# Masks added on TensorE, idle matmuls up front and earlier gates in an attention + expert kernel, with the loads of later batches re-hung to the new gates

## The chip, the cores and the metric

The kernel runs on one NeuronCore of a Trainium2 chip. The metric is the device time of one execution in microseconds (us); a profile's span of the same execution is about 1.6 us shorter. In the profile, PE is TensorE (it multiplies matrices into PSUM, its output memory), DVE is VectorE, ACT is ScalarE, and POOL is GpSimd. The granted clock is the share of TensorE's full clock that the profile shows. The DMA share is the time of all packets as a share of 16 DMA engines; it can exceed 1. The runs of the kernel before agree within 1%. Runs more than 1.5% above the fastest run of the same kernel are called slow.

## The reference, cut to what matters

Eight sentences (batches) of 576 positions, 8 heads of 64, pass through causal attention with a window of 64. The mean of the result over the positions picks one of eight experts for the whole sentence; the expert is a two-layer MLP with fp32 weights of 2 MB and 2 MB.

```python
scores = scale * np.matmul(q, k.transpose(0, 1, 3, 2))
mask = (rel >= 0) & (rel < window)                 # rel = row - column, window = 64
scores = np.where(mask, scores, -1000000000.0)
attn = ...softmax(scores)...;  x = attn @ v        # (B, S, H*D) = (8, 576, 512)
logits = x.mean(axis=1) @ w_gate                   # per sentence
e_idx = np.argmax(logits, axis=1)                  # one expert of 8 per sentence
h = np.maximum(x[mask] @ w1[e], 0.0)               # w1: 512 x 1024
out[mask] = gate_w * (h @ w2[e])                   # w2: 1024 x 512
```

So the weights of batch b can be loaded only when all of batch b's attention is done and its gate is known.

## The kernel before

Attention is cut into *units*: unit u = 5b + i is head pair i of batch b (i = 4 is the tail, positions 512 to 575). A unit has a transpose step T, a score step S and a value step A. The expert of a batch is cut into 18 *chunks*: nine of w1, nine of w2. Units and chunks are interleaved on TensorE. gate1(b) computes the logits, reads the index of the expert on GpSimd (POOL) and issues the loads of w1 and w2 there; gate2(b) broadcasts the gate's factor.

All loads of q, k, v, w1 and w2 are issued by POOL, because they change fp32 into a 2-byte type on the way. The Trainium skill, "DMA: Bandwidth & Descriptors", section "SWDGE vs HWDGE vs iDMA", says that a cast during DMA is tied to that path; the trace agrees in that all these loads are on one queue (q0, 30.94 MB). So POOL's program order is the order in which the loads start. In the trace they also landed in that order: behind gate 0, w1, w2, q and k had landed by 43.5, 49.2, 51.8 and 54.5 us (POOL's next issues wait for them).

```python
def load_qk(b, lo, hi): ...                 # 2 DMAs on nc.gpsimd, 512 KB each as stored in SBUF (2-byte)
def load_v(b, lo, hi): ...                  # 8 DMAs of 72 KB
def load_tail(b): ...                       # 2 DMAs of 64 KB

def unit_s(b, i):                           # scores; i < NP
    ... 8 matmuls into se, so ...
    nc.scalar.activation(out=pe, in_=se, func=AF.Exp, scale=scale)
    nc.scalar.activation(out=po, in_=so[:, :, 16:128], func=AF.Exp, scale=scale)
    nc.vector.tensor_tensor(out=pe, in0=pe, in1=mask, op=ALU.mult)
    nc.vector.tensor_tensor(out=po, in0=po, in1=mask[:, :, 0:112], op=ALU.mult)

def unit_a(b, i):                           # sums lb, values av: one PSUM buffer each
    ... ln(lb) and exp(-ln) on ScalarE, then on DVE:
    nc.vector.tensor_tensor_reduce(out=xm[:, i], in0=av, in1=rl, ..., accum_out=pool[b]...)

def gate1(b):
    ... 16 small matmuls gps <- pool, wg; glog, max, max_index on DVE ...
    nc.gpsimd.load(ereg, eidx[0:1, 0:1])
    nc.gpsimd.dma_start(out=w1t, in_=w1e[esl].squeeze(0))
    nc.gpsimd.dma_start(out=w2t, in_=w2e[esl].squeeze(0))
    ...

def moe(slot):                              # three slots a unit, LAG = 9
    t = slot - 3 * LAG
    want = min(len(todo), (t * NC) // (3 * NU)) if t > 0 else 0      # NC = 18, NU = 5
    ... issue chunks up to want ...

load_qk(1, 0, 8); load_v(1, 0, 4); load_tail(1)
unit_t(0, 0)
for u in range(n + 3):
    unit_t(u + 1); moe(3 * u); unit_s(u)
    if u >= 6 and (u - 6) % NU == 0:
        b = (u - 6) // NU
        gate1(b)
        if b == 0: load_qk(2, 0, 8); load_v(2, 0, 4); load_tail(2)
        if b + 3 < B: load_qk(b + 3, 0, 8); load_v(b + 3, 0, 4); load_tail(b + 3)
    if u >= 7 and (u - 7) % NU == 0: gate2((u - 7) // NU)
    moe(3 * u + 1); unit_a(u - 1); moe(3 * u + 2)
```

(Shortened: bounds are left out, units are named by number.) Note the load rule: behind gate b come q, k and v of batch b + 3, behind gate 0 also those of batch 2. A batch's data are thus asked for a whole batch before they are used.

The softmax here doesn't subtract the row's maximum and nothing guards it: scores larger than these inputs give would overflow.

Of the kernel before, what the change touches and what calls it, by code (L numbers as in the profile page):

```python
# [2 lines left out]
LAG=9  # L3
# [18 lines left out]
def kernel(  # L22
# [33 lines left out]
    NV = 3  # L56
# [30 lines left out]
    def load_v(b, lo, hi):  # L87
        vt = vbd[b % NV]
        for hh in range(2):
            for pr in range(lo, hi):  # L90
                nc.gpsimd.dma_start(  # L91
                    out=vt[64 * hh:64 * hh + 64, pr, :, 64 * hh:64 * hh + 64],
                    in_=v[b, 2 * pr + hh].rearrange("(j c) d -> c j d", c=64))

    nc.scalar.preload_act_table_set("natural_log_exp_and_others")
    ident = const.tile([128, 128], BF16)
    make_identity(nc, ident)
    load_qk(0, 0, 4)
    mb = const.tile([128, 4, 32], FP16)
    mt = const.tile([128, 2, 64], FP16)  # L100
    nc.vector.memset(mb, 1.0)
    nc.vector.memset(mt, 1.0)

    def zero(t, eng):
        for h in range(2):
            z = t[64 * h:64 * h + 64]
# [5 lines left out]

    zero(vbd[0], nc.vector)
    zero(kbd[0], nc.scalar)
    load_v(0, 0, 1)
    for p0 in (0, 64):
        m = mb[p0:p0 + 64]
        nc.gpsimd.affine_select(out=m, in_=m, compare_op=ALU.is_ge, fill=0.0,
                                base=0, pattern=[[1, 4], [4, 32]], channel_multiplier=-1)
        nc.gpsimd.affine_select(out=m, in_=m, compare_op=ALU.is_ge, fill=0.0,  # L120
                                base=63, pattern=[[-1, 4], [-4, 32]], channel_multiplier=1)
    load_v(0, 1, 2)
    load_qk(0, 4, 8)
    load_v(0, 2, 4)
    load_tail(0)
    for p0 in (0, 64):
        m = mt[p0:p0 + 64, 0]
        nc.gpsimd.affine_select(out=m, in_=m, compare_op=ALU.is_ge, fill=0.0,
                                base=-1, pattern=[[-1, 64]], channel_multiplier=1)
        m = mt[p0:p0 + 64, 1]  # L130
        nc.gpsimd.affine_select(out=m, in_=m, compare_op=ALU.is_ge, fill=0.0,
                                base=0, pattern=[[1, 64]], channel_multiplier=-1)
    mask = const.tile([128, 4, 128], FP16)
    for i in range(4):
        nc.vector.tensor_copy(out=mask[:, :, 32 * i:32 * i + 32], in_=mb)
    onesbd = const.tile([128, 128], FP16)
# [3 lines left out]
    ones1 = const.tile([1, 128], FP32)  # L140
    nc.vector.memset(ones1, 1.0)
    wg = const.tile([128, NP, E], FP32)
    nc.sync.dma_start(out=wg, in_=moe_w_gate.rearrange("(kb p) e -> p kb e", p=128))
    for i in range(2):
        zero(kbt[i].rearrange("q n (j d) -> q n j d", j=1), nc.scalar)
    zero(kbd[1], nc.scalar)
    zero(vbd[1], nc.scalar)
    zero(vbd[2], nc.scalar)

    tT = {}  # L150
    pt = {}
    xs = {}
# [3 lines left out]

    def unit_t(b, i):
        qm, km, qkt = qkv[b]
        if i < NP:
            tp = ps_t.tile([128, 2, 4, 128], BF16, tag="tp", name="tp")  # L160
            for (n, t) in ((0, qm), (1, km)):
                for r in range(4):
                    for hh in range(2):
                        p0 = 64 * hh
                        nc.tensor.transpose(tp[p0:p0 + 64, n, r], t[:, 2 * i + hh, ts(r, 64)], ident)  # L165
            qT = tpool.tile([128, 4, 128], BF16, tag="qT", name="qT", bufs=3)
            nc.vector.tensor_copy(out=qT, in_=tp[:, 0])  # L167
            kb = kbd[b % 2][:, i]
            for hh in range(2):
                p0 = 64 * hh  # L170
                (nc.vector.tensor_copy if KM == 'd' or (KM=='h' and hh==0) else nc.scalar.copy)(  # L171
# [3 lines left out]
        else:  # L175
            tp = ps_t.tile([128, NP, 128], BF16, tag="tp", name="tpt")
            for h in range(H):
                p0 = 64 * (h % 2)
                nc.tensor.transpose(tp[p0:p0 + 64, h // 2], qkt[:, h], ident)
# [280 lines left out]
```

## Time and profile before

| kernel before | value | view |
|---|---|---|
| time, 4 runs | 256.54 us median (255.12 to 257.44) | runs |
| span of the profiled run | 254.7 us | page |
| TensorE in work at 48-54 us | 0.64 of 6 us | table by stage |
| DMA share at 30-36 us | 0.01 | table by stage |
| gates 1 to 6 | 26.25 or 26.26 us apart | timeline |

The page's second part has the span in 40 slices of 6.4 us; digits are tenths of busy time, of the full clock (PEclk), and of the DMA engines.

```profile
PE   0487667059999999999999999999999999998893
...
PEclk9999955558999999999999999999999999999999
DMA  6999819999989999999999999999992199369923
```

Counted from 0: TensorE's slices 0 to 8 are not full, 7 is nearly empty and 8 half full, the clock stands at 0.5 in slices 5 to 8, and the DMA has one hole there, in slice 5. From slice 9 on TensorE is full until near the end. The table by stage (columns: window, its length, busy us of each engine with its instructions, granted clock, DMA share, GB/s) says the same in numbers:

```profile
30.00:36.00 6.00, 3.62 (x56) 2.79 (x52) 4.02 (x20) 2.38 (x6) 0.77 (x1) 0.68 0.01 3
...
48.00:54.00 6.00, 0.64 (x8) 0.40 (x8) 0.00 (x0) 0.00 (x0) 1.45 (x2) 0.50 1.54 192
...
90.00:96.00 6.00, 5.55 (x67) 3.24 (x66) 5.28 (x21) 3.11 (x8) 2.24 (x4) 1.00 1.96 173
```

Lines of the timeline (start, duration, engine, source line, operation, and in brackets the idle time before it and what ended it). The first is the issue of the first expert's w1; then batch 2's first transposes; then the first transposes of batches 3 and 4, which I call T(15) and T(20), with gate 2 between them:

```profile
35.22 0.77 POOL L294 DMA_DIRECT2D w1t<-in_moe_w_dram  x1 [8.63 <-DVE gw L305]
...
51.56 0.64 PE L165 MATMUL tp<-ident,qm 128*64 128x128 bf16 x8 [7.08 <-DMA qm<-in_q_dram]
...
54.21 0.64 PE L165 MATMUL tp<-ident,km 128*64 128x128 bf16 x8 [2.02 <-DMA km<-in_k_dram]
...
80.76 0.41 PE L165 MATMUL tp<-ident,qm 128*64 128x128 bf16 x8
...
93.13 0.55 PE L280 MATMUL gps<-wg,pool 128*1 128x8 f32 x16
...
107.02 0.41 PE L165 MATMUL tp<-ident,qm 128*64 128x128 bf16 x8
```

T(10) waits 7.1 us for q; T(15) and T(20) wait for nothing, their data have been there for over 12 us (k of batch 3 was issued at 57.4 and landed 8.8 us later, T(15) ran at 80.76; k of batch 4 landed at 94.2, T(20) ran at 107.02).

### The profile page before, as it was taken

How to read it: one execution, taken by the hardware profiler on the slowest of the kernel's cores; microseconds unless marked ns; L12 is line 12 of the kernel's file. 1: busy time of each engine (PE TensorE's matmuls, PEld its weight loads, DVE VectorE, ACT ScalarE, POOL GpSimd, SP SyncE). 2: the span in 40 equal slices, each digit the busy share in tenths (PEclk: the TensorE clock that was granted, in tenths of full speed). 3: DMA queues.
4: the chain of work that ended last, by engine and by line, in shares of the span. 5: the costliest groups of instructions: out<-in, count | busy, mean ns of one | idle time of the engine just before them, and what ended most of it. 6: DMA issues, size and time to landing. Idle time of an engine off the chain costs nothing.

```text
span 254.7 us, 5861 instructions
## 1 busy us (share of the span) xinstructions
PE 218.1 (86%) x2336; PEld 130.4 (51%) x2336; DVE 157.9 (62%) x444; ACT 132.1 (52%) x237; POOL 89.5 (35%) x128
## 2 busy tenths in 40 slices
PE   0487667059999999999999999999999999998893
PEld 0364455035565556565655665556555655554441
DVE  4569965136856796579747984698559854622411
ACT  8947644115565556646563656456555556522410
POOL 7995147158491129211931284125000200020000
PEclk9999955558999999999999999999999999999999
DMA  6999819999989999999999999999992199369923
GB/s 66 136 129 174 59 26 194 199 172 152 144 131 198 250 180 132 206 245 198 115 196 239 217 124 191 241 223 127 194 243 77 6 178 250 85 103 224 191 82 104
DMA packets 81995, 40.77 MB, mean 160 GB/s; under 512 B 48176, under 2 KB 73776, under 8 KB 81968
## 3 DMA queue, kind: packets, MB, share of 16 engines
q0 software_dynamic: 75552, 30.94, 102.4%
q1 hardware_dynamic: 6416, 9.46, 11.4%
q8 instruction: 18, 0.29, 0.4%
q14 instruction: 9, 0.07, 0.1%
HBM read 61.88 MB, written 9.44 MB: 280 GB/s over the span
## 4 chain that ended last, share of the span: by engine, by line
DMA 49%; PE 29%; POOL 10%; issue 5%; DVE 3%; ACT 2%; POOLq 1%; DVEq 0%
DMA km<-in_k_dram 35%; PE po L357 9%; PE ph L335 8%; DMA vbd_95<-in_v_dram 8%; DMA w2t<-in_moe_w_dram 7%; POOL vbd_94 L91 3%; PE tp L165 2%; POOL qm L76 2%; POOL w2t L295 1%; POOL qkt L83 1%; PE lb L231 1%; PE po L368 1%; PE ph L342 1%; PE av L235 1%; PE av L241 1%
## 5 line engine op out<-in xcount | busy, mean ns | idle before, releaser
L335 PE MATMUL ph<-xm,w1t 128*128 128x512 f16 x256 | 64.5, 386 | 0.9 <-DMA w1t<-in_moe_w_dram 0.9
L357 PE MATMUL po<-w2t,hm 128*128 128x512 f16 x256 | 62.7, 380 | 1.0 <-DMA w2t<-in_moe_w_dram 1.0
L249 DVE CUSTOM_DVE_ANT_0 xm<-av,rl 128x512 f16<-128x512 f32 x32 | 22.1, 692 | 46.7 <-ACT rl L248 46.7
L321 ACT ACTIVATE hm<-ph,gwb 128x512 f16<-128x512 f32 x32 | 22.0, 687 | 30.7 <-PE ph L335 30.5
L335 PEld LDWEIGHTS <-w1t 128*128 128x128 f16 x256 | 22.4, 99 | 22.5 <-DMA w1t<-in_moe_w_dram 1.2
L357 PEld LDWEIGHTS <-hm 128*128 128x128 f16 x256 | 21.7, 98 | 22.6 <-DMA w2t<-in_moe_w_dram 1.1
L91 POOL DMA_DIRECT2D vbd_95<-in_v_dram x24 | 17.7, 771 | 34.1 <-DMA w2t<-in_moe_w_dram 14.7
L165 PE MATMUL tp<-ident,qm 128*64 128x128 bf16 x256 | 14.6, 242 | 17.6 <-DMA qm<-in_q_dram 12.9
L201 ACT ACTIVATE pe<-se 128x512 f16<-128x512 f32 x32 | 19.0, 594 | 20.3 <-PE se L197 20.3
L323 DVE TENSOR_SCALAR hm<-ph,gwb 128x512 f16<-128x512 f32 x32 | 23.8, 743 | 5.9 <-PE ph L335 5.5
L294 POOL DMA_DIRECT2D w1t<-in_moe_w_dram x8 | 6.2, 774 | 55.0 <-DVE gw L305 54.9
L247 ACT ACTIVATE ln<-lb 128x512 f32<-128x512 f32 x32 | 19.1, 597 | 11.3 <-PE lb L237 11.0
L91 POOL DMA_DIRECT2D vbd_94<-in_v_dram x24 | 17.8, 774 | 18.8 <-DMA w2t<-in_moe_w_dram 6.1
L165 PEld LDWEIGHTS <-qm 128*64 128x64 bf16 x256 | 9.0, 118 | 26.6 <-DMA qm<-in_q_dram 14.3
L171 DVE COPY kbd_98<-tp 64x512 bf16<-64x512 bf16 x32 | 21.9, 683 | 0.2
L171 DVE COPY kbd_97<-tp 64x512 bf16<-64x512 bf16 x32 | 21.9, 683 | 0.2
L167 DVE COPY qT<-tp 128x512 bf16<-128x512 bf16 x32 | 13.4, 419 | 12.6 <-PE tp L165 12.6
L91 POOL DMA_DIRECT2D vbd_96<-in_v_dram x16 | 11.8, 762 | 26.1 <-DMA w2t<-in_moe_w_dram 11.5
L248 ACT ACTIVATE rl<-ln 128x512 f32<-128x512 f32 x32 | 20.2, 630 | 1.0
L231 PE MATMUL lb<-pe,onesbd 128*128 128x512 f16 x32 | 13.3, 414 | 6.9 <-DVE glog L286 4.6
L362 DVE COPY ob<-po 128x512 f32<-128x512 f32 x16 | 11.0, 689 | 13.0 <-PE po L357 12.8
L214 ACT ACTIVATE pp<-st 128x512 f16<-128x512 f32 x8 | 4.8, 597 | 26.1 <-PE st L211 26.1
(109 smaller groups left out, 363.7 us busy)
## 6 DMA issues: line engine op xcount, KB each, us to landing
w1t<-in_moe_w_dram POOLq DMA_DIRECT2D x8, 1024.0 KB, 9.4
w2t<-in_moe_w_dram POOLq DMA_DIRECT2D x8, 1024.0 KB, 16.3
out_dram<-ob SPq DMA_DIRECT2D x32, 256.0 KB, 6.5
qm<-in_q_dram POOLq DMA_DIRECT2D x7, 512.0 KB, 19.5
km<-in_k_dram POOLq DMA_DIRECT2D x7, 512.0 KB, 21.4
vbd_94<-in_v_dram POOLq DMA_DIRECT2D x24, 72.0 KB, 6.4
vbd_95<-in_v_dram POOLq DMA_DIRECT2D x24, 72.0 KB, 8.5
vbd_96<-in_v_dram POOLq DMA_DIRECT2D x16, 72.0 KB, 15.1
```

The costliest lines, as they stand in the source:

```text
L91: nc.gpsimd.dma_start(out=vt[64 * hh:64 * hh + 64, pr, :, 64 * hh:64 * hh + 64], in_=v[b, 2 * pr + hh].rearrange("(j c) d -> c j d", c=64))
L165: nc.tensor.transpose(tp[p0:p0 + 64, n, r], t[:, 2 * i + hh, ts(r, 64)], ident)
L171: (nc.vector.tensor_copy if KM == 'd' or (KM=='h' and hh==0) else nc.scalar.copy)(out=kb[p0:p0 + 64, :, p0:p0 + 64].rearrange("q j (p r) - ...
L201: nc.scalar.activation(out=pe, in_=se, func=AF.Exp, scale=scale)
L231: nc.tensor.matmul(out=lb, lhsT=onesbd, rhs=pe, start=True, stop=False, skip_group_check=True)
L247: nc.scalar.activation(out=ln, in_=lbf, func=AF.Ln)
L248: nc.scalar.activation(out=rl, in_=ln, func=AF.Exp, scale=-1.0)
L249: nc.vector.tensor_tensor_reduce(out=xm[:, i], in0=av.rearrange("q r p -> q (r p)"), in1=rl, scale=1.0, scalar=0.0, op0=ALU.mult, op1=ALU.add,
L321: nc.scalar.activation(out=o, in_=i, func=AF.Relu, scale=g)
L323: nc.vector.tensor_scalar(out=o, in0=i, scalar1=g, scalar2=0.0, op0=ALU.mult, op1=ALU.max)
L335: nc.tensor.matmul(out=ph, lhsT=w1t[:, kb, ts(ft, 128)], rhs=xm[:, kb], start=(kb == 0), stop=(kb == 3))
L357: nc.tensor.matmul(out=po, lhsT=hm[:, fb, ts(r, 128)], rhs=w2t[:, fb], start=(fb == 0), stop=(fb == 7))
```

## The change

Its intent: bring the first expert's weights forward, since all later loads queue behind them. Masks of the first five units become matmuls that add -30000 to masked scores ahead of the exponential (DVE is spared two multiplies a unit). Twelve idle matmuls at the start are to raise TensorE's clock. Gate 0 moves into its batch's last unit, gate 1 from unit 11 to the end of unit 9, and the first 12 chunks of expert 0 are placed by hand among units 7 to 9. The set-up is reordered. The loads hang on the gates, so their rule is rewritten too. Cut to its core:

```diff
-LAG=9
+WU=12;PB=5;KA=set(range(0));C1=12;A2=42
...
+    for i in range(WU):
+        nc.tensor.matmul(out=wps, lhsT=warm[:, 0:128], rhs=warm, start=True, stop=True)
...
+                if pm and j == 0:
+                    nc.tensor.matmul(out=se, lhsT=ident, rhs=maskb, start=True, stop=False,
+                                     skip_group_check=True)
...
-            nc.vector.tensor_tensor(out=pe, in0=pe, in1=mask, op=ALU.mult)
-            nc.vector.tensor_tensor(out=po, in0=po, in1=mask[:, :, 0:112], op=ALU.mult)
+            if b * NU + i >= PB:
+                nc.vector.tensor_tensor(out=pe, in0=pe, in1=mask, op=ALU.mult)
+                nc.vector.tensor_tensor(out=po, in0=po, in1=mask[:, :, 0:112], op=ALU.mult)
...
     def moe(slot):
-        t = slot - 3 * LAG
-        want = min(len(todo), (t * NC) // (3 * NU)) if t > 0 else 0
+        if slot < 30:
+            return
+        if slot < A2:
+            want = C1 + (NC - C1) * (slot - 30) // (A2 - 30)
+        else:
+            want = min(len(todo), NC + (slot - A2) * NC // (3 * NU))
...
+        if u == 4:
+            ops += [("S", 4), ("E", 4), ("A", 3), ("A", 4), ("Tp", 5), ("G1", 0), ("GR", 0),
+                    ("Te", 5), ("T", 6), ("S", 5), ("E", 5), ("G2", 0)]
...
+        if u == 9:
+            ops += [("C", 1), ("A", 9), ("C", 3), ("G1", 1), ("GR", 1), ("C", 2), ("T", 10), ("G2", 1)]
...
+        g = u > 11 and (u - 6) % NU == 0
...
+    LD = {0: lambda: loads(2), 1: lambda: loads(3), 2: lambda: (loads(4), qk(5)),
+          3: lambda: (vt(5), loads(6)), 4: lambda: loads(7), 5: lambda: None,
+          6: lambda: None, 7: lambda: None}
```

LD[b] is what is loaded right behind gate b's weights. From slot 42 (unit 14) on, the pace of the chunks is the same as before: (slot - 27) * 18 / 15 and 18 + (slot - 42) * 18 / 15 are equal.

More of the change, by code (lines that the diff above doesn't have):

```diff
@@ L87, in load_v, with zero @@
     def load_v(b, lo, hi):
-        vt = vbd[b % NV]
-        for hh in range(2):
-            for pr in range(lo, hi):
+        for pr in range(lo, hi):
+            for hh in range(2):
+                p0 = 64 * hh
                 nc.gpsimd.dma_start(
-                    out=vt[64 * hh:64 * hh + 64, pr, :, 64 * hh:64 * hh + 64],
+                    out=vbd[b % NV][p0:p0 + 64, pr, :, p0:p0 + 64],
                     in_=v[b, 2 * pr + hh].rearrange("(j c) d -> c j d", c=64))
     nc.scalar.preload_act_table_set("natural_log_exp_and_others")
-    ident = const.tile([128, 128], BF16)
-    make_identity(nc, ident)
-    load_qk(0, 0, 4)
-    mb = const.tile([128, 4, 32], FP16)
-    mt = const.tile([128, 2, 64], FP16)
-    nc.vector.memset(mb, 1.0)
-    nc.vector.memset(mt, 1.0)
-    def zero(t, eng):
+    def zero(t, eng, lo=0, hi=None):
         for h in range(2):
-            z = t[64 * h:64 * h + 64]
+            z = t[64 * h:64 * h + 64, lo:hi]
             z = z.rearrange("q n j d -> q (n j) d")[:, :, 64 - 64 * h:128 - 64 * h]
@@ L111, in zero @@
                 eng.memset(z.bitcast(U32), 0)
+    ident = const.tile([128, 128], BF16)
+    mb = const.tile([128, 4, 32], FP16)
+    mt = const.tile([128, 2, 64], FP16)
+    onesbd = const.tile([128, 128], FP16)
+    ones1 = const.tile([1, 128], FP32)
+    warm = const.tile([128, 512], BF16)
+    mask = const.tile([128, 4, 128], FP16)
+    maskb = const.tile([128, 4, 128], BF16)
+    mtb = const.tile([128, 2, 64], BF16)
+    wg = const.tile([128, NP, E], FP32)
+    load_qk(0, 0, 2)
+    nc.vector.memset(warm, 0.0)
@@ new lines @@
+    nc.vector.memset(ident, 0.0)
+    nc.vector.memset(mb, 1.0)
+    nc.vector.memset(mt, 1.0)
+    nc.gpsimd.affine_select(out=ident, in_=ident, compare_op=ALU.not_equal, fill=1.0,
+                            base=0, pattern=[[-1, 128]], channel_multiplier=1)
+    nc.sync.dma_start(out=wg, in_=moe_w_gate.rearrange("(kb p) e -> p kb e", p=128))
+    wps = ps_m.tile([128, 512], FP32, tag="mo", name="wps")
+    for i in range(WU):
+        nc.tensor.matmul(out=wps, lhsT=warm[:, 0:128], rhs=warm, start=True, stop=True)
@@ L113 @@
+    m = mb[0:64]
+    nc.gpsimd.affine_select(out=m, in_=m, compare_op=ALU.is_ge, fill=0.0,
+                            base=0, pattern=[[1, 4], [4, 32]], channel_multiplier=-1)
+    nc.gpsimd.affine_select(out=m, in_=m, compare_op=ALU.is_ge, fill=0.0,
+                            base=63, pattern=[[-1, 4], [-4, 32]], channel_multiplier=1)
+    load_qk(0, 2, 8)
+    zero(kbd[0], nc.scalar)
     zero(vbd[0], nc.vector)
-    zero(kbd[0], nc.scalar)
     load_v(0, 0, 1)
-    for p0 in (0, 64):
-        m = mb[p0:p0 + 64]
-        nc.gpsimd.affine_select(out=m, in_=m, compare_op=ALU.is_ge, fill=0.0,
-                                base=0, pattern=[[1, 4], [4, 32]], channel_multiplier=-1)
-        nc.gpsimd.affine_select(out=m, in_=m, compare_op=ALU.is_ge, fill=0.0,
-                                base=63, pattern=[[-1, 4], [-4, 32]], channel_multiplier=1)
+    m = mt[0:64, 0]
@@ L122 @@
+    nc.gpsimd.affine_select(out=m, in_=m, compare_op=ALU.is_ge, fill=0.0,
+                            base=-1, pattern=[[-1, 64]], channel_multiplier=1)
+    m = mt[0:64, 1]
+    nc.gpsimd.affine_select(out=m, in_=m, compare_op=ALU.is_ge, fill=0.0,
+                            base=0, pattern=[[1, 64]], channel_multiplier=-1)
     load_v(0, 1, 2)
-    load_qk(0, 4, 8)
+    load_tail(0)
     load_v(0, 2, 4)
-    load_tail(0)
-    for p0 in (0, 64):
-        m = mt[p0:p0 + 64, 0]
-        nc.gpsimd.affine_select(out=m, in_=m, compare_op=ALU.is_ge, fill=0.0,
-                                base=-1, pattern=[[-1, 64]], channel_multiplier=1)
-        m = mt[p0:p0 + 64, 1]
-        nc.gpsimd.affine_select(out=m, in_=m, compare_op=ALU.is_ge, fill=0.0,
-                                base=0, pattern=[[1, 64]], channel_multiplier=-1)
@@ L133 @@
-    mask = const.tile([128, 4, 128], FP16)
-    for i in range(4):
-        nc.vector.tensor_copy(out=mask[:, :, 32 * i:32 * i + 32], in_=mb)
-    onesbd = const.tile([128, 128], FP16)
     nc.vector.memset(onesbd, 0.0)
@@ L139 @@
     nc.vector.memset(onesbd[64:128, 64:128], 1.0)
-    ones1 = const.tile([1, 128], FP32)
     nc.vector.memset(ones1, 1.0)
-    wg = const.tile([128, NP, E], FP32)
-    nc.sync.dma_start(out=wg, in_=moe_w_gate.rearrange("(kb p) e -> p kb e", p=128))
-    for i in range(2):
-        zero(kbt[i].rearrange("q n (j d) -> q n j d", j=1), nc.scalar)
+    nc.vector.tensor_copy(out=mb[64:128], in_=mb[0:64])
+    for i in range(4):
+        nc.vector.tensor_copy(out=mask[:, :, 32 * i:32 * i + 32], in_=mb)
+    nc.vector.tensor_scalar(out=maskb, in0=mask, scalar1=-1.0, scalar2=30000.0,
+                            op0=ALU.add, op1=ALU.mult)
+    zero(vbd[1], nc.vector)
     zero(kbd[1], nc.scalar)
-    zero(vbd[1], nc.scalar)
-    zero(vbd[2], nc.scalar)
+    zero(kbt[0].unsqueeze(2), nc.scalar)
+    zero(kbt[1].unsqueeze(2), nc.scalar)
     tT = {}
     pt = {}
+    sps = {}
     xs = {}
@@ L155, with unit_tp @@
     wts = {}
+    tps = {}
     def unit_t(b, i):
+        unit_tp(b, i)
+        unit_te(b, i)
+    def unit_tp(b, i):
         qm, km, qkt = qkv[b]
         if i < NP:
-            tp = ps_t.tile([128, 2, 4, 128], BF16, tag="tp", name="tp")
+            if b == 0 and i % 2:
+                tp = ps_m.tile([128, 2, 4, 128], BF16, tag="mo", name="tp")
+            else:
+                tp = ps_t.tile([128, 2, 4, 128], BF16, tag="tp", name="tp")
             for (n, t) in ((0, qm), (1, km)):
@@ L165, in unit_t, with unit_te @@
                         nc.tensor.transpose(tp[p0:p0 + 64, n, r], t[:, 2 * i + hh, ts(r, 64)], ident)
+            tps[b, i] = tp
+        else:
+            tp = ps_t.tile([128, NP, 128], BF16, tag="tp", name="tpt")
+            for h in range(H):
+                p0 = 64 * (h % 2)
+                nc.tensor.transpose(tp[p0:p0 + 64, h // 2], qkt[:, h], ident)
+            tps[b, i] = tp
+    def unit_te(b, i):
+        tp = tps.pop((b, i))
+        if i < NP:
             qT = tpool.tile([128, 4, 128], BF16, tag="qT", name="qT", bufs=3)
@@ L170, in unit_t @@
                 p0 = 64 * hh
-                (nc.vector.tensor_copy if KM == 'd' or (KM=='h' and hh==0) else nc.scalar.copy)(
+                (nc.scalar.copy if hh and b * NU + i in KA else nc.vector.tensor_copy)(
                     out=kb[p0:p0 + 64, :, p0:p0 + 64].rearrange("q j (p r) -> q j p r", r=4),
@@ L175, in unit_t @@
         else:
-            tp = ps_t.tile([128, NP, 128], BF16, tag="tp", name="tpt")
-            for h in range(H):
-                p0 = 64 * (h % 2)
-                nc.tensor.transpose(tp[p0:p0 + 64, h // 2], qkt[:, h], ident)
             qT = tpool.tile([128, NP, 64], BF16, tag="qTt", name="qTt")
@@ L193, in unit_s @@
             so = ps_s.tile([128, 4, 128], FP32, tag="so", name="so")
+            pm = b * NU + i < PB
             for j in (0, 2, 4, 6, 1, 3, 5, 7):
@@ L196, in unit_s, with unit_e @@
                 dst = (so if j % 2 else se)[:, :, 16 * j:16 * j + w]
-                nc.tensor.matmul(out=dst, lhsT=kb[:, j], rhs=qT[:, :, 16 * j:16 * j + w],
-                                 start=True, stop=True, skip_group_check=True)
+                if pm and j == 0:
+                    nc.tensor.matmul(out=se, lhsT=ident, rhs=maskb, start=True, stop=False,
+                                     skip_group_check=True)
+                if pm and j == 1:
+                    nc.tensor.matmul(out=so[:, :, 16:128], lhsT=ident, rhs=maskb[:, :, 0:112],
+                                     start=True, stop=False, skip_group_check=True)
+                nc.tensor.matmul(out=dst, lhsT=kb[:, j], rhs=qT[:, :, 16 * j:16 * j + w],
+                                 start=not pm, stop=True, skip_group_check=True)
+            sps[b, i] = (se, so)
+        else:
+            sp = ps_s.tile([128, NP, 2, 64], FP32, tag="se", name="st")
+            pm = b * NU + i < PB
+            if pm:
+                nc.tensor.matmul(out=sp, lhsT=ident,
+                                 rhs=mtb.unsqueeze(1).broadcast_to([128, NP, 2, 64]),
+                                 start=True, stop=False, skip_group_check=True)
+            for n in range(NP):
+                nc.tensor.matmul(out=sp[:, n, 0], lhsT=kbd[b % 2][:, n, 7], rhs=qT[:, n],
+                                 start=not pm, stop=True, skip_group_check=True)
+                nc.tensor.matmul(out=sp[:, n, 1], lhsT=kbt[b % 2][:, n], rhs=qT[:, n],
+                                 start=not pm, stop=True, skip_group_check=True)
+            sps[b, i] = sp
+    def unit_e(b, i):
+        if i < NP:
+            se, so = sps.pop((b, i))
             pe = apool.tile([128, 4, 128], FP16, tag="pe", name="pe", bufs=3)
@@ L202, in unit_s @@
             nc.scalar.activation(out=po, in_=so[:, :, 16:128], func=AF.Exp, scale=scale)
-            nc.vector.tensor_tensor(out=pe, in0=pe, in1=mask, op=ALU.mult)
-            nc.vector.tensor_tensor(out=po, in0=po, in1=mask[:, :, 0:112], op=ALU.mult)
+            if b * NU + i >= PB:
+                nc.vector.tensor_tensor(out=pe, in0=pe, in1=mask, op=ALU.mult)
+                nc.vector.tensor_tensor(out=po, in0=po, in1=mask[:, :, 0:112], op=ALU.mult)
             pt[b, i] = (pe, po)
         else:
-            sp = ps_s.tile([128, NP, 2, 64], FP32, tag="se", name="st")
-            for n in range(NP):
-                nc.tensor.matmul(out=sp[:, n, 0], lhsT=kbd[b % 2][:, n, 7], rhs=qT[:, n],
-                                 start=True, stop=True, skip_group_check=True)
-                nc.tensor.matmul(out=sp[:, n, 1], lhsT=kbt[b % 2][:, n], rhs=qT[:, n],
-                                 start=True, stop=True, skip_group_check=True)
+            sp = sps.pop((b, i))
             pp = apool.tile([128, NP, 2, 64], FP16, tag="pp", name="pp")
             nc.scalar.activation(out=pp, in_=sp, func=AF.Exp, scale=scale)
-            nc.vector.tensor_tensor(
-                out=pp, in0=pp,
-                in1=mt.unsqueeze(1).broadcast_to([128, NP, 2, 64]), op=ALU.mult)
+            if b * NU + i >= PB:
+                nc.vector.tensor_tensor(
+                    out=pp, in0=pp,
+                    in1=mt.unsqueeze(1).broadcast_to([128, NP, 2, 64]), op=ALU.mult)
             pt[b, i] = pp
@@ L299, in gate1, with gate_w @@
                                 scalar2=None, op0=ALU.mult)
+        gates[b] = (glog, gnm)
+    def gate_w(b):
+        glog, gnm = gates[b]
         gex = gpool.tile([1, E], FP32, tag="gex", name="gex")
@@ L390, in moe @@
     def moe(slot):
-        t = slot - 3 * LAG
-        want = min(len(todo), (t * NC) // (3 * NU)) if t > 0 else 0
+        if slot < 30:
+            return
+        if slot < A2:
+            want = C1 + (NC - C1) * (slot - 30) // (A2 - 30)
+        else:
+            want = min(len(todo), NC + (slot - A2) * NC // (3 * NU))
         while done[0] < want:
@@ L395, in moe, with loads @@
             done[0] += 1
+    def loads(b):
+        if b < B:
+            load_qk(b, 0, 8)
+            load_v(b, 0, 4)
+            load_tail(b)
+    n = len(units)
+    ops = []
+    for u in range(n + 3):
+        b = u // NU
+        if u == 4:
+            ops += [("S", 4), ("E", 4), ("A", 3), ("A", 4), ("Tp", 5), ("G1", 0), ("GR", 0),
+                    ("Te", 5), ("T", 6), ("S", 5), ("E", 5), ("G2", 0)]
+            continue
+        if u == 5:
+            ops += [("T", 7), ("S", 6), ("E", 6), ("A", 5)]
+            continue
+        if u == 6:
+            ops += [("T", 8), ("S", 7), ("E", 7), ("A", 6)]
+            continue
+        if u == 7:
+            ops += [("T", 9), ("C", 1), ("S", 8), ("E", 8), ("C", 1), ("A", 7), ("C", 1)]
+            continue
+        if u == 8:
+            ops += [("C", 1), ("S", 9), ("E", 9), ("C", 1), ("A", 8), ("C", 1)]
+            continue
+        if u == 9:
+            ops += [("C", 1), ("A", 9), ("C", 3), ("G1", 1), ("GR", 1), ("C", 2), ("T", 10), ("G2", 1)]
+            continue
+        ops += [("T", u + 1), ("M", 3 * u), ("S", u)]
+        g = u > 11 and (u - 6) % NU == 0
+        if g:
+            ops += [("G1", b - 1)]
+        ops += [("E", u)]
+        if g:
+            ops += [("GR", b - 1)]
+        ops += [("M", 3 * u + 1)]
+        if u != 10:
+            ops += [("A", u - 1)]
+        if g:
+            ops += [("G2", b - 1)]
+        ops += [("M", 3 * u + 2)]
@@ L397, with qk, vt @@
+    fn = {"T": unit_t, "Tp": unit_tp, "Te": unit_te, "S": unit_s, "E": unit_e, "A": unit_a}
+    def qk(b):
+        load_qk(b, 0, 8)
+    def vt(b):
+        load_v(b, 0, 4)
+        load_tail(b)
+    LD = {0: lambda: loads(2), 1: lambda: loads(3), 2: lambda: (loads(4), qk(5)),
+          3: lambda: (vt(5), loads(6)), 4: lambda: loads(7), 5: lambda: None,
+          6: lambda: None, 7: lambda: None}
     with tc.manual_schedule():
-        load_qk(1, 0, 8)
-        load_v(1, 0, 4)
-        load_tail(1)
@@ L401 @@
         unit_t(0, 0)
-        n = len(units)
-        for u in range(n + 3):
-            if u + 1 < n:
-                unit_t(*units[u + 1])
-            moe(3 * u)
-            if u < n:
-                unit_s(*units[u])
-            if u >= 6 and (u - 6) % NU == 0:
-                b = (u - 6) // NU
-                gate1(b)
-                if b == 0:
-                    for c in (2,):
-                        load_qk(c, 0, 8)
-                        load_v(c, 0, 4)
-                        load_tail(c)
-                if b + 3 < B:
-                    load_qk(b + 3, 0, 8)
-                    load_v(b + 3, 0, 4)
-                    load_tail(b + 3)
-            if u >= 7 and (u - 7) % NU == 0:
-                gate2((u - 7) // NU)
-            moe(3 * u + 1)
-            if 1 <= u <= n:
-                unit_a(*units[u - 1])
-            moe(3 * u + 2)
+        loads(1)
@@ new lines @@
+        zero(vbd[2], nc.gpsimd)
+        for (op, x) in ops:
+            if op == "M":
+                moe(x)
+            elif op == "G1":
+                if x < B:
+                    gate1(x)
+                    LD[x]()
+            elif op == "C":
+                for _ in range(x):
+                    todo[done[0]]()
+                    done[0] += 1
+            elif op == "GR":
+                if x < B:
+                    gate_w(x)
+            elif op == "G2":
+                if x < B:
+                    gate2(x)
+            elif 0 <= x < n:
+                fn[op](*units[x])
+            if (op, x) == ("S", 1):
+                nc.vector.tensor_copy(out=mt[64:128], in_=mt[0:64])
+                nc.vector.tensor_scalar(out=mtb, in0=mt, scalar1=-1.0, scalar2=30000.0,
+                                        op0=ALU.add, op1=ALU.mult)
```

## The prediction

> **What bounds the kernel now.**
> 1. Up to 60 us: waiting. The table by stage shows TensorE busy 0.64 of 6 us at 48-54. Batch 2's first transposes wait 7.1 us for q and 2.0 for k (waits of TensorE). Before that the DMA idles: at 30-36 its share is 0.01, from the landing of batch 1's last loads (29) to the issue of expert weights w1(0) at 35.2. The gate was late: sums at 30.9, glog copied at 33.4, behind copies and mask multiplies (2.6) on DVE. The granted clock is 0.50 at 36-54.
> 2. 60-222: TensorE. Busy over 98% of 100-200; one batch takes 26.26 us (gate matmuls at 93.13, 119.39, 145.65).
> 3. The tail: gate 7 at 221.6, w2(7) lands 242.2.
> The DMA is nearly as full in stage 2: w1, w2, q, k and v of a batch with its outputs take about 26.5 us.
>
> **What the change does.** Masks as matmuls for five units: DVE 3.3 us a unit falls to 2.5; TensorE gains two 512-column matmuls a unit (0.21 us each warm). Twelve idle matmuls (0.43 cold) overlap the first loads. The Trainium skill, "TensorE: Matmul & The Clock Gate", part 1, gives about 3.4 us of activity before full clock; the trace agrees roughly (54.8-59.3 dense, then full rate). Gate 0 moves to about 24, but w1(0) sits on POOL behind batch 1's loads and a memset, so I put its issue at 27.5 (35.2 before). Expert 0's first 12 chunks fill the wait for batch 2. Gate 1 moves from 66.9 to about 48. But qk(3) now come after w(1), and batch 4 after gate 2's w(2): a prefetch is one batch shallower until gate 3.
>
> **On the critical path.** From unit 14 on the chunk pacing is the same as before, so only what unit 14's and unit 19's transposes gain counts.
> - T(15), 80.8 before: it waits for k(3). DMA, with the durations of before: issue 27.5, +19 k(2), +5.4 v(2), +12 w(1), +5.5 qk(3), +2 outputs: about 71. TensorE would be there at 66.
> - Gate 2: +12.4, about 84; w1(2) issued at 86, with the DMA idle since about 77.
> - T(20), 107.0 before: TensorE wants it 13.9 us after gate 2, but w(2) and qk(4) take 19 to 22 us from issue. Landing about 106; a new stall of some 7 us, then a cold restart (about 2 us).
> The 10 us lead at T(15) is given back at T(20). From there the gate broadcast placed right after a unit's sums must wait for ln to read the same PSUM bank (about 0.6 us a batch lost), the earlier glog copy saves 0.44.
>
> **Predicted: 256 us** (8 in 10: 250 to 262.5); faster by over 2% 0.2, within 0.65, slower 0.15.
>
> **What would show it.** Right: w1(0) issued at 26-30; no long TensorE gap at 45-55; T(15) at 69-74; among TensorE's waits k or q of batch 4, 5 us or more at 97-107, granted clock 0.5 after it; a DMA trough at 77-86; T(20) within 3 us of 107; then 26.3 us a batch. Wrong: T(20) at 102 or earlier (gain kept), or w1(0) still after 32.
>
> **What would make it wrong.** DMA faster than the durations of before : T(15) and T(20) move with it, and 5 us are possible. Or the early steps slower: mask constants late on POOL, gate 1 after 52, a clock that stays low through units 5-13; then over 260.

## The result, and the profile after

Measured: 272.86 us median of 4 runs (270.27 to 274.62), against 256.54 for the kernel before. The ratio is 1.061, 95% interval 1.050 to 1.071. Ratios here are the mean time of one kernel's fast runs over that of the other's fast runs of the same rounds, so not quite the ratio of the medians quoted. The profiled run (274.62, span 273.0) was the slowest of the four; the three fast ones are at 270 or more as well, and a fast trace of a kernel that is identical up to gate 3 (f_gate3 below) has gates 0 to 4 at the same times to within 0.6 us. The third hole below is seen in this run alone; f_gate3 shows the same kind of hold-up one batch later, in a fast run.

```profile
PE   7495598979439995089999999489999999998983
...
PEclk9888569988968999669999999979999999999998
DMA  5999299969995099999299999999998079639913
```

Slices are 6.8 us here. The hole of before (slices 7 and 8 there) is gone, but there are three new ones in TensorE's row: slices 10 and 11, 15 and 16, and 25. The DMA's row is half full in slice 12 and empty in 13, shortly before the second. TensorE's waits, summed (total, times, longest):

```profile
PE tp L185 <- DMA qm<-in_q_dram: 15.0, 3, 7.7
PE tp L185 <- DMA km<-in_k_dram: 6.9, 3, 2.7
PE ph L388 <- DMA w1t<-in_moe_w_dram: 5.6, 2, 4.8
```

And the timeline, with the same events as before: w1(0), T(15), gate 2, the issue of w1(2), T(20), and the third hole.

```profile
30.84 0.77 POOL L343 DMA_DIRECT2D w1t<-in_moe_w_dram  x1 [3.13 <-DVE qT L198]
...
76.53 0.64 PE L185 MATMUL tp<-ident,qm 128*64 128x128 bf16 x8 [5.05 <-DMA qm<-in_q_dram]
...
79.92 0.64 PE L185 MATMUL tp<-ident,km 128*64 128x128 bf16 x8 [2.75 <-DMA km<-in_k_dram]
...
92.55 0.54 PE L329 MATMUL gps<-wg,pool 128*1 128x8 f32 x16
...
95.03 0.77 POOL L343 DMA_DIRECT2D w1t<-in_moe_w_dram  x1 [12.78 <-PE av L290]
...
114.17 0.64 PE L185 MATMUL tp<-ident,qm 128*64 128x128 bf16 x8 [7.71 <-DMA qm<-in_q_dram]
...
116.91 0.64 PE L185 MATMUL tp<-ident,km 128*64 128x128 bf16 x8 [2.11 <-DMA km<-in_k_dram]
...
178.66 1.71 PE L388 MATMUL ph<-xm,w1t 128*128 128x512 f16 x4 [4.79 <-DMA w1t<-in_moe_w_dram]
```

The table by stage shows what went on between gate 1's loads and gate 2's:

```profile
84.00:90.00 6.00, 6.00 (x62) 3.52 (x61) 3.98 (x9) 4.43 (x9) 0.00 (x0) 1.00 0.11 22
90.00:96.00 6.00, 5.51 (x75) 3.49 (x73) 5.26 (x22) 3.76 (x8) 0.97 (x2) 1.00 0.02 4
...
108.00:114.00 6.00, 0.00 (x0) 0.00 (x0) 0.00 (x0) 0.00 (x0) 0.73 (x1) 0.72 1.31 233
```

The DMA stands idle at 84-96 (share 0.11 and 0.02, where before had 1.96 in 90-96), because by the load rule nothing more is issued before gate 2 is known. Then TensorE stands idle at 108-114, because everything comes at once, weights first. The clearest account is the time of each gate's matmul (from the timelines; difference is after minus before):

| gate | 0 | 1 | 2 | 3 | 4 | 5 | 6 | 7 | end |
|---|---|---|---|---|---|---|---|---|---|
| before | 30.66 | 66.88 | 93.13 | 119.39 | 145.65 | 171.91 | 198.17 | 221.56 | 254.7 |
| after | 28.07 | 54.08 | 92.55 | 130.88 | 157.10 | 189.94 | 216.15 | 239.50 | 273.0 |
| difference | -2.6 | -12.8 | -0.6 | +11.5 | +11.5 | +18.0 | +18.0 | +17.9 | +18.3 |

The change does what it was made for: gate 1 comes 12.8 us earlier. All of it is lost by gate 2, another 12.1 us by gate 3, and 6.6 between gates 4 and 5. Elsewhere a batch takes 26.2 us as before.

### The profile page after: what moved, and what is told of

Read it like the earlier page. It is cut to its first block, busy times and chain, and to the rows that moved or that the text cites. A ratio compares the mean times of both kernels' runs of the same rounds, so it can differ in the third digit from the quotient of the medians.

```text
span 273.0 us, 5890 instructions
## 1 busy us (share of the span) xinstructions
PE 226.4 (83%) x2357; PEld 133.7 (49%) x2357; DVE 158.3 (58%) x443; ACT 128.2 (47%) x233; POOL 90.1 (33%) x125
## 4 chain that ended last, share of the span: by engine, by line
PE 40%; DMA 37%; DVE 11%; POOL 4%; issue 3%; ACT 2%; POOLq 0%
DMA km<-in_k_dram 17%; DMA w2t<-in_moe_w_dram 13%; PE ph L388 11%; PE po L410 9%; DMA w1t<-in_moe_w_dram 4%; PE tp L185 4%; DMA vbd_94<-in_v_dram 4%; PE po L421 2%; DVE kbd_98 L202 2%; DVE hm L376 2%; PE se L231 2%; PE av L284 1%; PE lb L280 1%; PE lb L286 1%; POOL qm L76 1%
## 5 line engine op out<-in xcount | busy, mean ns | idle before, releaser
L410 PE MATMUL po<-w2t,hm 128*128 128x512 f16 x256 | 64.2, 388 | 0.9 <-DMA w2t<-in_moe_w_dram 0.9
L410 PEld LDWEIGHTS <-hm 128*128 128x128 f16 x256 | 22.1, 99 | 23.3 <-issue 1.3
L202 DVE COPY kbd_97<-tp 64x512 bf16<-64x512 bf16 x32 | 21.9, 684 | 0.3
L202 DVE COPY kbd_98<-tp 64x512 bf16<-64x512 bf16 x32 | 21.9, 684 | 0.2
L185 PE MATMUL tp<-ident,km 128*64 128x128 bf16 x256 | 14.2, 240 | 6.9 <-DMA km<-in_k_dram 6.9
```

The costliest lines, as they stand in the source:

```text
L185: nc.tensor.transpose(tp[p0:p0 + 64, n, r], t[:, 2 * i + hh, ts(r, 64)], ident)
L202: (nc.scalar.copy if hh and b * NU + i in KA else nc.vector.tensor_copy)(out=kb[p0:p0 + 64, :, p0:p0 + 64].rearrange("q j (p r) -> q j p r ...
L410: nc.tensor.matmul(out=po, lhsT=hm[:, fb, ts(r, 128)], rhs=w2t[:, fb], start=(fb == 0), stop=(fb == 7))
```

## The experiments

**Theory 1.** The rule of the loads alone lost the time: with it, q, k and v of batch b + 2 (not b + 3) stand behind the 2 MB of weights (1 MB each of w1 and w2 in SBUF) of gate b, with only three units between gate 2 and T(20). **Theory 2 (rival).** The rest of the change loses it: masks on TensorE, the mixed order of the early units, a falling clock. A second rival, within theory 1, was that the DMA's total work bounds, so that its order hardly matters.

Ten kernels were run, each with three timed rounds beside the kernel before on the same chip; all gave correct results.

| kernel | median us (4 runs) | ratio to before, 95% |
|---|---|---|
| the change | 272.86 | 1.061 (1.050 to 1.071) |
| a_deep | 253.58 | 0.984 (0.975 to 0.992) |
| a_qk3 | 251.27 | 0.973 (0.967 to 0.979) |
| a_qk4 | 258.89 | 1.010 (1.005 to 1.014) |
| b_shallow | 291.15 | 1.138 (1.134 to 1.141) |
| d_pb0 | 252.19 | 0.986 (0.979 to 0.994) |
| d_wu0 | 254.76 | 0.992 (0.986 to 0.997) |
| d_oldorder | 254.37 | 0.995 (0.991 to 0.999) |
| a_qk34 | 248.72 | 0.970 (0.965 to 0.975) |
| f_gate3 | 273.87 | 1.072 (1.066 to 1.078) |
| best_plain | 250.60 | 0.979 (0.971 to 0.986) |

The medians are over all four runs; the ratios leave out the slow ones (one run of the change, of a_deep and of d_wu0, two of a_qk3).

### Only the loads: a_deep, and the reverse, b_shallow

a_deep is the changed kernel with the load rule of before:

```diff
-    LD = {0: lambda: loads(2), 1: lambda: loads(3), 2: lambda: (loads(4), qk(5)),
-          3: lambda: (vt(5), loads(6)), 4: lambda: loads(7), ...
+    LD = {0: lambda: (loads(2), loads(3)), 1: lambda: loads(4), 2: lambda: loads(5),
+          3: lambda: loads(6), 4: lambda: loads(7), ...
```

> The changed kernel with only the table of loads put back to the depth of before: q, k and v of batches 2 and 3 behind gate 0, of batch b+3 behind gate b. Theory 1 (the load order alone lost the time, because batches 3 and 4 stand behind two megabytes of weights): the 7 to 10 us TensorE waits for q and k of batches 3 and 4 vanish, the 4.8 us wait for w1(4) too; instead one short wait (up to 6 us) for w1(1) at unit 14, since w1(1) now stands behind batch 3; gates from gate 2 on 26.3 us apart; 247 to 252 us, so ahead of before. Theory 2 (the rest of the change - masks on TensorE, mixed order of the early units, a clock that falls - costs the time): still above 262 us.

Measured: 253.58 us, 19 us less than the change, by one table of loads. The waits for batches 3 and 4 and the one for w1(4) are gone. Gates 2 to 6 follow at 26.2 us. What is left is one wait for w1(1), which now stands behind batch 3. Its gates 2 and 3, and this wait:

```profile
90.52 0.55 PE L329 MATMUL gps<-wg,pool 128*1 128x8 f32 x16
...
116.73 0.55 PE L329 MATMUL gps<-wg,pool 128*1 128x8 f32 x16
...
PE ph L388 <- DMA w1t<-in_moe_w_dram: 5.8, 1, 5.8
```

Theory 2 falls. The same data are loaded in both kernels, so as a cause of this loss the rival that only the DMA's total counts falls too. The time is a little above my 247 to 252. The clock was 0.55 of full at 78-84, after the 5.8 us wait; that this makes the difference is not shown.

b_shallow is the kernel before with only the new load rule:

```diff
-                if b == 0:
-                    for c in (2,):
-                        load_qk(c, 0, 8); load_v(c, 0, 4); load_tail(c)
-                if b + 3 < B:
-                    load_qk(b + 3, 0, 8); load_v(b + 3, 0, 4); load_tail(b + 3)
+                if b < 3:
+                    load_qk(b + 2, 0, 8); load_v(b + 2, 0, 4); load_tail(b + 2)
+                if b == 2:
+                    load_qk(5, 0, 8)
+                if b == 3:
+                    load_v(5, 0, 4); load_tail(5)
+                if b in (3, 4):
+                    load_qk(b + 3, 0, 8); load_v(b + 3, 0, 4); load_tail(b + 3)
```

> The kernel before with only the changed kernel's order of loads (batch 2 behind gate 0, 3 behind gate 1, 4 and q, k of 5 behind gate 2, v of 5 and batch 6 behind gate 3). Theory 1: since gate 1 comes only at 66.9 here, the loss is larger than in the changed kernel: waits for q and k of batches 3 and 4 of 8 us or more each, gates 1-2 and 2-3 36 to 40 us apart, 275 to 290 us. Theory 2: within 2 per cent of before, 252 to 261 us.

Measured: 291.15 us, 1.138 times before; gates 1 to 2 and 2 to 3 are 39.1 and 40.4 us apart. The total is 1 us over my 275 to 290. Gates 1, 2 and 3, and the wait for q alone:

```profile
65.96 0.55 PE L280 MATMUL gps<-wg,pool 128*1 128x8 f32 x16
...
105.04 0.55 PE L280 MATMUL gps<-wg,pool 128*1 128x8 f32 x16
...
145.48 0.55 PE L280 MATMUL gps<-wg,pool 128*1 128x8 f32 x16
...
PE tp L165 <- DMA qm<-in_q_dram: 31.2, 4, 9.4
```

So the load rule by itself loses 35 us in the old kernel and 19 in the new one; that the new kernel's earlier gate 1 softens it is my reading, not tested alone. Theory 1 is shown from both sides.

### One stall at a time: a_qk4 and f_gate3

a_qk4 leaves batch 3 behind gate 1's weights, and moves only q and k of batch 4 (and from there keeps the rule b + 3):

```diff
+    LD = {0: lambda: loads(2), 1: lambda: (loads(3), qk(4)), 2: lambda: (vt(4), loads(5)),
+          3: lambda: loads(6), 4: lambda: loads(7), ...
```

> The changed kernel with only q and k of batch 4 moved from gate 2 to gate 1, and then b+3. Batch 3 still stands behind w(1). Theory 1: the wait for batch 3 at unit 14 stays (T(15) complete at about 80, as in the changed kernel), the wait for batch 4 at 105 to 117 and the one for w1(4) at 174 to 179 vanish: gates 1 to 2 still 38 us apart, then 26.3; 255 to 259 us. Theory 2: above 265 us.

Measured: 258.89 us. T(15) still waits, 4.7 us for q and 2.7 for k, and its k part starts at 80.67; gates 1 to 2 are 38.6 us apart. Gates 2 to 3 are 26.2 apart instead of 38.3. As expected, the first stall stayed and the other two went (w1 waits sum to 2.3 us), though gates 3 to 6 are 27.1 to 27.9 apart and not 26.3. The first stall:

```profile
77.32 0.64 PE L185 MATMUL tp<-ident,qm 128*64 128x128 bf16 x8 [4.72 <-DMA qm<-in_q_dram]
...
80.67 0.64 PE L185 MATMUL tp<-ident,km 128*64 128x128 bf16 x8 [2.71 <-DMA km<-in_k_dram]
```

f_gate3 is aimed at the third stall, which the prediction did not have. In the changed kernel gate 4's matmul ran at 157.10, but its weights were issued 10 us later. POOL was still issuing the loads behind gate 3, the last two v each when an earlier transfer had landed:

```profile
157.10 0.55 PE L329 MATMUL gps<-wg,pool 128*1 128x8 f32 x16
...
163.88 0.73 POOL L91 DMA_DIRECT2D vbd_94<-in_v_dram  x1 [1.87 <-DMA km<-in_k_dram]
166.09 0.69 POOL L83 DMA_DIRECT2D qkt<-in_q_dram  x1 [1.48 <-DMA vbd_94<-in_v_dram]
166.76 0.69 POOL L83 DMA_DIRECT2D qkt<-in_k_dram  x1
167.53 0.77 POOL L343 DMA_DIRECT2D w1t<-in_moe_w_dram  x1
```

f_gate3 moves v of batch 6 from gate 3 to gate 4:

```diff
-          3: lambda: (vt(5), loads(6)), 4: lambda: loads(7), 5: lambda: None,
+          3: lambda: (vt(5), qk(6)), 4: lambda: (vt(6), loads(7)), 5: lambda: None,
```

> The changed kernel with one thing moved: v of batch 6 from gate 3 to gate 4, so that POOL is done with gate 3's loads before gate 4 is known (in the changed kernel w1(4) was issued at 167.5, gate 4's matmul having run at 157.1; POOL was still issuing batch 6's v as earlier transfers landed). If that is the cause of the third stall (wait of 4.8 us for w1(4), gates 4 to 5 32.8 us apart): w1(4) issued by 160, the wait under 1 us, gates 4 to 5 26 to 27.5 us apart, the stalls for batches 3 and 4 unchanged (gates 1-2 and 2-3 38 apart), total 263 to 268 us. If the DMA's own backlog and not POOL's order holds w1(4) up: the wait stays within 2 us of 4.8 and the total at 270 or more.

Measured: 273.87 us; the total missed my range. Gates 4 to 5 are 26.2 us apart and w1(4) was issued at 159.54, as soon as gate 4 was known: its cause was POOL's order. But the wait moved one batch on. w1(5) was issued only at 191.94, behind v of 6 and all of batch 7, though gate 5 had run at 183.29, and gates 5 to 6 are now 30.7 apart:

```profile
159.54 0.76 POOL L343 DMA_DIRECT2D w1t<-in_moe_w_dram  x1 [4.32 <-PE av L290]
...
183.29 0.55 PE L329 MATMUL gps<-wg,pool 128*1 128x8 f32 x16
...
191.94 0.79 POOL L343 DMA_DIRECT2D w1t<-in_moe_w_dram  x1
...
202.74 1.89 PE L388 MATMUL ph<-xm,w1t 128*128 128x512 f16 x4 [2.67 <-DMA w1t<-in_moe_w_dram]
```

A load taken out of one gate's queue is not gone; it lengthens the next one's. In the kernels whose loads run further ahead (a_deep, a_qk4 and the two below) no wait for w1 after gate 3 is over 1.5 us.

### What the other parts are worth: d_pb0, d_wu0, d_oldorder

These three undo one part each in a_deep. d_pb0 sets `PB=0` (no mask matmuls), d_wu0 sets `WU=0` (no idle matmuls), and d_oldorder drops the hand-placed units 4 to 9 and the new pace:

```diff
-        if u == 4: ... if u == 9: ...   (the six hand-placed branches)
-        g = u > 11 and (u - 6) % NU == 0
+        g = u >= 6 and (u - 6) % NU == 0
-        if slot < 30: return ... A2 ...
+        t = slot - 27
+        want = min(len(todo), (t * NC) // (3 * NU)) if t > 0 else 0
```

> a_deep with no mask on TensorE (the mask multiplies of units 0 to 4 back on DVE). Theory M (the masks on TensorE bring gate 0 forward): each of the five units takes about 0.8 us longer on DVE, gate 0's matmul comes 2 to 4 us later than a_deep's 28.3, w1(0) too, and since the loads from then on follow one another, the total grows by as much: 255 to 258 us against a_deep's 253.6. Rival N (the five units are bound by the chain sums - ln - reciprocal - xm through the one PSUM bank of av, not by DVE's total): gate 0 within 1 us of 28.3, total within 1 us of a_deep.

> a_deep without the twelve idle matmuls at the start. If they help: early units stay at half rate longer and gate 0 comes over 1 us later than 28.3. If not (the trace of the changed kernel shows half rate again at 12.0 to 15.1 while the unit before had waited for k until 11.08): gate 0 within 0.5 us, total within 1 us of a_deep.

> a_deep with the order of units 4 to 9, the place of gates 0 and 1 and the pace of the expert chunks as before; masks on TensorE, idle matmuls, the set-up order and the deep loads stay. Theory D (in the deep order the DMA bounds the start, so early chunks and an early gate 1 only wait for w1(1)): gate 0 at 29 to 31, gate 1 at 62 to 65, TensorE waits for batch 2 of about 10 us again, total within 2 us of a_deep (252 to 256). Rival: the mixed order is what gains, then 256 us or more.

Measured: 252.19, 254.76 and 254.37 us, all within 1.4 us of a_deep's 253.58, with overlapping intervals (by the ratios, up to some 2% either way is not excluded). w1(0) was issued at 30.49 without mask matmuls, at 31.87 without idle ones, and at 31.09 in a_deep itself; kernels that are the same up to that point (a_qk3, a_qk4, a_qk34) issued it at 32.09, 31.99 and 32.82. So neither part is shown to bring gate 0 forward; the differences are no larger than those between equal kernels. d_wu0 falls between its two cases: gate 0 came 0.8 us later. For d_pb0 the rival N of its expectation holds for gate 0 (27.99 against 28.32; the total, 1.4 us lower, is just outside its 1 us): DVE was busy 12.3 us of the 17 from 11 to 28, against 9.1 in a_deep, and gate 0 came no later. So the five units are not bound by DVE's total. The trace of the changed kernel shows what they wait for ahead of gate 0:

```profile
22.73 0.69 DVE L298 CUSTOM_DVE_ANT_0 xm<-av,rl 128x512 f16<-128x512 f32 x1 [1.25 <-ACT rl L297]
...
23.49 0.38 PE L284 MATMUL av<-pe,vbd_94 128*128 128x128 f16 x4 [1.02 <-DVE pool L298]
...
24.10 0.60 ACT L296 ACTIVATE ln<-lb 128x512 f32<-128x512 f32 x1 [0.91 <-PE lb L286]
...
25.39 0.69 DVE L298 CUSTOM_DVE_ANT_0 xm<-av,rl 128x512 f16<-128x512 f32 x1 [1.95 <-ACT rl L297]
...
26.14 0.21 PE L306 MATMUL al<-pp,vbd_94 128*128 128x64 f16 x1 [1.88 <-DVE pool L298]
```

A(2), A(3) and A(4) run one after another, about 2.7 us each: sums, ln, reciprocal, xm, and only then is the one PSUM buffer of av free for the next. With two A steps back to back, DVE waits for ScalarE and not the other way round.

d_oldorder has its gate 1 at 64.50 instead of a_deep's 54.32, and yet gate 2 comes at 90.72 against 90.52:

```profile
90.72 0.55 PE L329 MATMUL gps<-wg,pool 128*1 128x8 f32 x16
```

Theory D holds by its marks (gate 0 at 30.23; 9.2 and 2.1 us of waiting for batch 2). In the deep order the early chunks end in the wait for w1(1). The intervals of the two ratios only just overlap, though, so a difference of about 1% is possible. One more thing shows here: w1(0) was issued at 34.03, against 31.09 in a_deep and 35.22 before. So, as far as one trace each can say, most of its gain came with the hand-placed order, not with the masks or the idle matmuls.

### Both at once: a_qk3, a_qk34, best_plain

If the early gate 1 is worth something, w1(1) must not stand behind all of batch 3, and T(15) must not stand behind w(1). a_qk3 puts only q and k of batch 3 ahead of gate 1; a_qk34 moves v of batch 4 back too:

```diff
+    LD = {0: lambda: (loads(2), qk(3)), 1: lambda: (vt(3), loads(4)), 2: lambda: loads(5),     # a_qk3
+    LD = {0: lambda: (loads(2), qk(3)), 1: lambda: (vt(3), qk(4)), 2: lambda: (vt(4), loads(5)),  # a_qk34
+          3: lambda: loads(6), 4: lambda: loads(7), ...
```

> The changed kernel with q and k of batch 3 put behind gate 0 (ahead of w1(1)), v of batch 3 and batch 4 behind gate 1, then b+3 as before. Theory 1: no wait for q and k of batch 3 or 4, w1(1) about 6 us earlier than in a_deep and so no wait for it either; 245 to 250 us. Theory 2: above 262 us. If the DMA total is what bounds (theory 1b), a_qk3 and a_deep come out within 1 us of each other.

> a_qk3 with v of batch 4 moved behind gate 2's weights as well, so that w1(2) is 5 us earlier in the DMA's order. a_qk3 lost 5.8 us between gates 2 and 3 (32.1 apart, w1 waits of 3.0). If that loss is the place of w1(2) in the order: gates 2 to 3 26 to 28.5 us apart, total 246 to 250 us. If the DMA's total work is the bound by then, the wait moves to v of batch 4 or to w1(3) and the total stays at 250 to 252 us.

Measured: a_qk3 251.27 us, a little over its 245 to 250. Its gate 2 comes at 83.97, 9.2 us ahead of before, but gates 2 to 3 are 32.1 apart, with a wait of 3.0 us for w1(2). Its profiled run is one of its two slow runs, as long as a_deep's (span 252.0 both), so whether its fast runs (250.13 and 248.06) had this wait is not shown. a_qk3 against a_deep was meant to test the second rival; their intervals overlap, so that pair does not decide. a_qk34: 248.72 us, gates 2 to 3 are 26.2 apart, and the waits for w1 sum to 0.6 us:

```profile
84.65 0.55 PE L329 MATMUL gps<-wg,pool 128*1 128x8 f32 x16
...
110.87 0.55 PE L329 MATMUL gps<-wg,pool 128*1 128x8 f32 x16
```

It is 3.0% faster than before (interval 0.965 to 0.975) and has the lowest time found, but it is not separated from a_qk3's 0.973. Its slowest run (249.88) is below every run of a_deep (250.09 and up) and of the three kernels with a_deep's loads on the same chip (251.61 and up). So the order of the loads mattered here too, although the amount did not change. Later gates of a_qk34 are up to 26.8 us apart, a little above TensorE's 26.2: I take it that past gate 2 there is not much left to gain from order alone.

best_plain is a_qk34 with `WU=0;PB=0`:

> a_qk34 (248.7 us) without masks on TensorE and without idle matmuls. d_pb0 was not slower than a_deep and d_wu0 by about 1 us at most. If the two parts do nothing for the time also in this order of loads: within 1.5 us of a_qk34, 247 to 250 us. If they matter once the loads no longer stall: 251 us or more.

Measured: 250.60 us, between the two cases of its expectation; ratio 0.979 (0.971 to 0.986) against a_qk34's 0.970 (0.965 to 0.975). The intervals overlap. Whether the two parts are worth about 1% once the loads fit stays open; the runs do not show it.

## Why the prediction was wrong, point by point

Much of the mechanism was right. The prediction said that T(15) would wait for k of batch 3, that the DMA would then stand idle until gate 2, and that T(20) would wait some 7 us for batch 4, followed by low clock. The waits were 5.05 and 2.75 us at T(15), 7.71 and 2.11 at T(20), the idle stretch 84-96, the clock 0.50 at 114-120. But the prediction also kept a lead of 10 us at T(15), which the wait at T(20) would only give back. In fact the lead was nearly gone at T(15) (its k part at 79.9, against 80.8 for T(15) before), so the wait at T(20) was a loss against the kernel before; and one stall was missing. The result, 272.86 us, is far outside 250 to 262.5. The prediction had named a case for over 260, "gate 1 after 52", and gate 1 came at 54.08.

- **"T(15) ... about 71": 79.9.** This is the step that failed. Its sum had these terms: w1(0) issued at 27.5, in fact at 30.84 (+3.3); from there to batch 2's last tail 24.4, in fact 24.9 (+0.5: it landed at 55.7); from there to k of batch 3 19.5, in fact 24.2 (+4.7). The first term was too small because I took gate 0 to come at 24, from DVE's total alone; the A steps run one after another and it came at 28.07. The last term was too small in part because I took gate 1 to come at 48, in time to keep the DMA busy. It came at 54.08 (4.1 of these 6 us are gate 0's; w1(0) landed at 38.7, and the first chunk ran at 42.2), w1(1) was issued at 56.61, and the queue had run dry by then: share 0.61 at 54-60. That issue is only 0.9 us after the last tail. The other 3.8 are that k of batch 3 landed 23.3 us after w1(1)'s issue, where I had allowed 19.5 from a full queue; the same loads of batch 2 took 20.3, without the four output stores issued from 56.2 to 72.8. How much is the empty queue and how much the stores is open.
- **"Gate 2: +12.4": 12.6.** From T(15)'s k transposes at 79.92 to 92.55. Right.
- **"w(2) and qk(4) take 19 to 22 us from issue": 21.9.** From 95.03 to 116.91. Right. So of the 10.9 us by which T(20) came late (116.9, not 106), 9.0 were there when w1(2) was issued (95.03, not 86), because T(15) was late. In other words, the chain gate, weights, next batch, gate was seen, but each late link is passed on in full, and I gave it the earliest time at each link.
- **"From there ... 26.3 us a batch": not for batch 4.** Gates 4 to 5 took 32.8 us. POOL issues in order, and batch 6's loads behind gate 3 held w1(4) back from gate 4 (157.10) to 167.53. f_gate3 shows the cause, and that the delay is passed to the next batch when it is taken away here. The prediction had no such term.
- **"a cold restart (about 2 us)".** Gates 2 to 3 took 38.3 us; less 26.2 and the waits of 9.8 that leaves 2.3. Right.
- **The masks and the idle matmuls.** I counted DVE's saving (3.3 to 2.5 us a unit) toward gate 0. d_pb0 shows no gain from it. The idle matmuls did raise the clock: transposes at 5.75 took 0.41 us for eight, against 0.64 in the kernel before and in d_wu0. But TensorE then waited until 11.08 for k, and the clock was 0.50 at 12-15. The Trainium skill, "TensorE: Matmul & The Clock Gate", part 1, gives about 3.4 us of activity for full clock; the trace agrees (first matmul at 1.39, full rate by 5.75).
- **The gate's broadcast.** TensorE did wait 0.49 us there in most batches, but in sum it was of no weight: undisturbed gates are 26.22 us apart against 26.26.

Adding up in the profile: the prediction put T(20) at 106 and so the end about where before had it; T(20) 10.9 us later and the missing stall of 6.6 make 17.5 of the 18.3 us that were lost against before.

What stays open: why the changed kernel and a_deep spread over 4 to 5 us from run to run (270.3 to 274.6; 250.1 to 255.5) while the kernel before stays within 2.3.

## What to carry to other kernels

When loads hang on an event such as a gate, moving the event earlier is no reason to ask for less ahead: check, for every batch, how much stands in front of it in the queue when it is asked for and how long the compute leaves it, here 22 us against 13.9. A lead gained at the front of a chain is kept only if the next link's data arrive early as well, so rebalance the order of the loads (q and k before weights, v after) instead of only delaying them. And when predicting such a chain, add up the latest of each link's conditions, not the earliest.

## What the Trainium skill lacked or had wrong

- "TensorE: Matmul & The Clock Gate", section "Why this matters for your kernels", says to leave no idle gaps of over about 3 us between bursts of matmuls. That is not enough here. The page's section "A second HAM failure mode: psum-queue depth-cycling" does tell of a kernel whose short, frequent idles brought the clock down, but gives no measure. In the changed kernel the clock fell to 0.50 at about 25.3 us (mean 0.64 in 25 to 26) although no gap since the first score matmul at 11.4 had been longer than 1.9 us; TensorE had been busy 0.43, 0.51 and 0.26 us in the three microseconds from 22 to 25. In the kernel before it fell shortly after 32, after 0.54, 0.44, 1.00 and 0.21 us in the four from 28 to 32. So in these two cases a stretch of about half or less busy was enough; other cases are not shown.
- "DMA: Bandwidth & Descriptors" has no figure for how far POOL can run ahead of its own transfers. Here it issued six v loads behind q and k without a pause (or four v behind w1, w2, q and k, at 95.03), eight loads in all, and then waited for an earlier load to land before each further one (idle 1.87 us until k landed, at 163.88). Whether the chip or the semaphores of this program set the eight is not shown. An instruction that depends on a gate, placed behind such loads, was held up for 8 us beyond the gate (157.10 to 167.53, 10.4 us; in f_gate3 157.07 to 159.54, 2.5).
- No page that I used warns that a load behind a gate is held up by the loads of the gate before it; "Perfetto Trace Analysis" would be the place. Its cost here was the third stall, 6.6 us.
